# Set-up of a fused recurrence and highway layer: identity folded into the raw weights, diagonals on GpSimd, weight scaling on ScalarE, y parts of the last outputs issued ahead, another order list

## The chip, the cores and the metric

The kernel runs on one core of one Trainium2 chip. The metric is the device time of one execution in microseconds. A profiled execution also gives a span, from the first to the last recorded instruction; the time is a little longer than the span.

Names in the profile: PE is TensorE (PEld its weight loads), DVE is VectorE, ACT is ScalarE, POOL is GpSimd, SP is SyncE, whose queue here issues all the large transfers.

## The reference

Two layers follow each other on 4 x 6336 tokens of 256 channels, all in float32:

```python
sig = 1 / (1 + exp(-f_logit))
f = lower_bound + (1 - lower_bound) * sig
for t in range(S):                       # per batch row, h starts at 0
    h = f[:, t] * h + (1 - f[:, t]) * x[:, t]
    y[:, t] = h
H = maximum(y @ w_h, 0)
T = 1 / (1 + exp(-(y @ w_t + b_t)))
out = T * H + (1 - T) * y
```

With u = 1 - sig = sigmoid(-f_logit) and c = 1 - lower_bound, per channel, f is 1 - c u and (1 - f) x is c u x. Since the recurrence is linear, the kernel scans b = u x instead of c u x; its y is then the true one divided by c, and c has to come back in the weights (both matrices are multiplied by c, row by row) and in the output.

The output is y + T (H - y). With H - y = max(y w_h - y, -y), the kernel takes w_h with the identity subtracted, so that a matmul gives y (w_h - I), and builds d = max(that, -c y), then d T, then the output as c y + d T.

## The kernel before

**Tiling.** The 25344 tokens are cut into 28 units, numbered 0 to 27, of 2, 2, 4, then 23 times 8, then 4 and 2 blocks of 128 tokens. Two halves of 128 channels (h or m, 0 and 1) are worked on separately. For each unit there are these steps, each a function `do_<letter>`:

- `l`, `x`: load the logits and x by SP (line 244), 1 MB each for a unit of 8 blocks
- `u`: u = sigmoid(-l), ScalarE (L256), tokens on partitions
- `b`: bv = u x, on GpSimd, or on VectorE where the token carries a `v` (L264)
- `i`: transposes of u into PSUM, TensorE (L271); `f`: f = 1 - c u out of PSUM, on ScalarE (L282) or, with `v`, on VectorE (L280)
- `p`: transposes of bv, TensorE (L291); `s`: the scan, VectorE (L308), which takes its start value from the scan of the unit before
- `z`, `g`: the two matrix products, TensorE (L320, with repeated blocks through the helper at L114)
- `t`: T = sigmoid(z + b_t), ScalarE (L333); `d`: max, VectorE (L337); `e`: d T, GpSimd or with `v` VectorE (L343)
- `o`: output in PSUM, tokens on partitions again, TensorE: c y by a product with a diagonal matrix `diag` (L365), plus d T by a product with the identity (L366)
- `c`: copy out of PSUM, ScalarE (L378) or with `v` VectorE (L376); `w`: store by SP (L382)

A token such as `b3.1v:0` means: step b of unit 3, part 1, on VectorE, in buffer slot 0. A step `k*3` is three matmuls of zeros on TensorE whose result nobody reads (L125, L114).

**Order.** Nothing chooses the order at run time. The long string `order` lists all steps; they are issued in that order and pinned (`pin`), so that each engine, SP too, works through its part of the list from front to back, waiting where an input or a buffer is not ready. An instruction that waits holds up all that stands behind it on its engine.

**Set-up steps.** `wt`, `wh` load the weights into `w_raw`; `pc`, `pb` turn lower_bound and b_t onto partitions with TensorE; `cc` makes c and -c (`ncc`) on VectorE; `dg` makes `diag` (c on the diagonal) and `ndiag` (-c on the diagonal), four VectorE instructions; `WT` scales w_t by c into `w_sb`, two VectorE instructions; `WH` does the same for w_h and adds `ndiag` to the two square parts on its diagonal, four VectorE instructions; `cb` copies b_t. A variant `WTa` for ScalarE exists and is not used.

**Shared port.** `shared` (L178) is called for `b`, `e`, `dg`, `WT`, `WH`: the next such GpSimd instruction is made to wait for the last such VectorE instruction before it in the list.

The PSUM has slots a0 and a1 of one bank (transposes `i` and `p`) and b0, b1, b2 of two banks (products, outputs).

Of the kernel before, what the change touches and what calls it, by code (L numbers as in the profile page):

```python
# [58 lines left out]
p6.1:0 i8.1:1 z5.0:1 f8.1:0 x10:1 e4.1 t5.0:0 g5.1:0 i7.1:1 b8.0:1 s6.1 i7.0:0 d5.0:1 z5.1:1 l12:2 f7.1:1 p7.1:1 d5.1
f7.0:2 t5.1 b8.1 g6.0:2 p7.0:0 e5.1 k*3:0 o4.1:1 s7.1:0 z6.0:0 d6.0:2 s7.0 u9:1 b9.0:2 g6.1:2 c4.1:3 d6.1 i9.0:1  # L60
t6.0:1 b9.1 o4.0:1 u11:2 i9.1:0 f9.0v:1 c4.0:2 w4.0 e6.0v f9.1:2 g7.1:0 z6.1:2 k*3:1 e5.2v i8.0:1 z7.0:1 e5.0v t6.1
w4.1 f8.0:3 p8.1:0 d7.1:0 t7.0:0 g7.0:2 e6.1 p8.0:1 b11.0:3 o5.0:0 u10:1 c5.0:0 w5.0 x12:2 o5.1:1 c5.1:1 w5.1 s8.1:1
i11.1:0 z7.1:0 f11.1:0 s8.0 b11.1 l13:0 d7.0 p9.0:1 i10.1:0 z8.0:1 e6.2 b10.1:1 g8.1:2 t7.1 f10.1:3 p9.1:0 s9.0:2
o6.1:0 x13:0 i10.0:1 d8.1:1 s9.1 g8.0:2 t8.0:1 u12:3 o6.0:1 f10.0:1 c6.1:0 c6.0:2 b10.0 e7.0 i11.0:1 w6.0 p10.0:0 w6.1
f11.0:2 z8.1:0 t8.1 z9.0:1 t9.0:0 d8.0 g9.0:2 s10.0:3 i12.0:1 p10.1:0 l14:1 f12.0:1 d9.0:2 o7.0:0 g9.1:1 c7.0:1 x14:1
w7.0 s10.1 u13:1 o7.1:2 c7.1:3 w7.1 b12.0:2 l17:0 p11.0:1 d9.1 s11.0:0 z9.1:0 t9.1 i12.1:0 b12.1 l15:2 z10.1:1 g10.1:2
e8.0 t10.1:2 e9.0v b13.0:1 z10.0:0 f12.1:2 p11.1:1 b13.1 t10.0 o8.1:1 d10.1:0 p12.1:0 c8.1:0 o8.0:2 s11.1 u14:2
g10.0:0 d10.0 c8.0:2 b14.1:3 i13.1:1 e10.0 f13.1:0 g11.1:1 b14.0 z11.1:0 s12.1:1 d11.1:1 w8.0 t11.1:0 x15:0 w8.1
# [5 lines left out]
p15.1:1 s15.1 c12.1:1 b17.1:2 f16.0:2 z14.1:0 z14.0:2 p16.0:0 s16.0:1 c12.0:3 t14.1:1 t14.0 g14.0:1 d14.0 i16.1:1
w11.1 l19:1 u18:3 x18:0 b17.0 e14.0 g15.1:0 d15.1:2 z15.0:2 i17.1:0 x19:3 f16.1:0 b18.0:3 p16.1:1 f17.1:1 b18.1 l20:2
s16.1 o13.1:1 t15.0:0 p17.0:0 g15.0:0 w12.1 d15.0 c13.1:0 u19:1 b19.1:1 o13.0:2 p17.1:1 z15.1:1 c13.0:2 z16.0:0
s17.1:2 t15.1 t16.0:1 z16.1:2 s17.0 g16.0:1 w13.1 t16.1 i18.0:1 d16.0:0 g16.1:0 o14.0:2 i18.1:0 f18.0:0 d16.1 e15.0v
o14.1:1 p18.0:1 s18.0:3 u20:2 w12.0 z17.0:0 c14.0:0 c14.1:1 f18.1:1 g17.0:2 d17.0:1 z17.1:1 b19.0 t17.0:0 i19.1:0
# [344 lines left out]
```

## Time and profile before

| | us |
|---|---|
| median of 3 runs | 207.75 (207.75 to 211.6) |
| profiled execution, its own time | 207.88 |
| its span | 206.1 |

| engine | busy us | share of the span | instructions |
|---|---|---|---|
| TensorE | 192.6 | 93% | 1837 |
| VectorE | 194.5 | 94% | 159 |
| ScalarE | 191.9 | 93% | 192 |
| GpSimd | 173.8 | 84% | 93 |

The DMA moved 78.68 MB, at a mean of 382 GB/s over the span. The granted TensorE clock was 0.995 of full speed.

How to read it: busy time is the union of an engine's recorded instructions. Matmuls are pipelined and their recorded ends are modelled, so a full TensorE row does not mean that it could do no more. In a timeline a row gives start, length, engine, line, operation, output and inputs with their shape, and, in brackets, the idle time before it and what ended that. In the rows that group instructions, the numbers are the busy time, the mean of one in ns, and the idle time before them. "SPq" is SP's queue of transfers.

### The profile page before, as it was taken

The page shows a single profiled execution, that of the slowest core. Times are in us where ns is not written, and L with a number is a line of the kernel's source. Part 1 is how long each engine was busy: PE and PEld are TensorE (multiplying, and loading weights), DVE is VectorE, ACT ScalarE, POOL GpSimd, SP SyncE. Part 2 cuts the span into 40 slices and gives each one's busy share as a digit, 9 for nine tenths or more (in the row PEclk, how much of TensorE's full clock was granted, in tenths as well). Part 3 has the DMA queues.
Part 4 walks back from the last instruction along what each step waited for, and adds up shares of the span by engine and source line. Part 5 has one row for each costly group of instructions (what it writes and reads, how often), then busy time and mean ns, then how long its engine had stood idle before and what let it go on. Part 6 is the DMA issues. An engine that isn't in the chain of part 4 may idle for free.

```text
span 206.1 us, 4635 instructions
## 1 busy us (share of the span) xinstructions
PE 192.6 (93%) x1837; PEld 133.8 (65%) x1837; DVE 194.5 (94%) x159; ACT 191.9 (93%) x192; POOL 173.8 (84%) x93
## 2 busy tenths in 40 slices
PE   7798799799998999999999999999999999999991
PEld 2366465566685776676577576677758758776770
DVE  0899999999999999999899999999999999999972
ACT  4369999999999999999999999999999999999891
POOL 3036989789979997999999999799899999998840
PEclk9999999999999999999999999999999999999997
DMA  6999999999999999999999999999999999725396
GB/s 196 370 424 422 411 418 423 409 423 417 414 423 408 429 417 426 423 420 413 425 424 416 433 411 417 429 415 418 407 422 422 414 392 378 286 104 204 138 382 248
DMA packets 16125, 78.68 MB, mean 382 GB/s; under 512 B 1764, under 2 KB 2536, under 8 KB 10216
## 3 DMA queue, kind: packets, MB, share of 16 engines
q1 hardware_dynamic: 16096, 78.39, 93.6%
q8 instruction: 14, 0.23, 0.4%
q14 instruction: 7, 0.06, 0.1%
q10 hardware_dynamic: 8, 0.00, 0.0%
HBM read 52.43 MB, written 25.95 MB: 380 GB/s over the span
## 4 chain that ended last, share of the span: by engine, by line
PE 53%; ACT 14%; DMA 13%; DVE 10%; issue 6%; POOL 2%; SPq 1%; ACTq 0%; DVEq 0%; POOLq 0%
DMA x<-in_x_dram 9%; DVE y L308 8%; PE op L366 7%; PE bT L291 7%; PE op L365 7%; PE g L320 7%; PE z L320 6%; PE uT L271 6%; PE g L114 6%; PE z L114 6%; ACT o L378 4%; ACT f L282 4%; DMA out_dram<-o 4%; ACT t L333 3%; POOL bv L264 2%
## 5 line engine op out<-in xcount | busy, mean ns | idle before, releaser
L264 POOL TENSOR_TENSOR bv<-u,x 128x1024 bf16<-128x1024 f16 (+1 forms) x49 | 100.9, 2085 | 16.9 <-DVE bt L207 10.7
L308 DVE TENSOR_TENSOR_SCAN y<-f,y,bT 128x1024 bf16<-128x1024 f16 (+5 forms) x54 | 106.8, 1989 | 0.2 <-PE bT L291 0.2
L343 POOL TENSOR_TENSOR d<-d,t 128x512 bf16<-128x512 bf16 (+3 forms) x33 | 73.3, 2234 | 9.6 <-DVE d L343 4.2
L337 DVE SCALAR_TENSOR_TENSOR d<-y,ncc,g 128x1024 bf16<-128x1024 bf16 (+2 forms) x56 | 63.1, 1137 | 1.5 <-PE g L320 1.0
L333 ACT ACTIVATE t<-z,bt 128x1024 bf16<-128x1024 f32 (+2 forms) x56 | 58.9, 1088 | 1.3 <-PE z L114 0.7
L282 ACT ACTIVATE f<-uT,ncc 128x1024 f16<-128x1024 f16 (+2 forms) x51 | 55.4, 1098 | 3.4 <-PE uT L271 2.2
L378 ACT COPY o<-op 128x1024 f32<-128x1024 f32 (+2 forms) x55 | 52.1, 984 | 2.4 <-PE op L366 1.6
L256 ACT ACTIVATE u<-l 128x2048 f16<-128x2048 f32 (+2 forms) x28 | 49.8, 1781 | 2.8 <-DMA l<-in_f_logit_dram 2.7
L366 PE MATMUL op<-ident_b,d 128*128 128x128 bf16 x396 | 49.5, 219 | 0.6 <-DVE d L343 0.6
L365 PE MATMUL op<-diag,y 128*128 128x128 f16 x396 | 49.7, 219 | 0.1
L366 PEld LDWEIGHTS <-d 128*128 128x128 bf16 x396 | 44.0, 113 | 3.2 <-DVE d L343 0.7
L365 PEld LDWEIGHTS <-y 128*128 128x128 bf16 x396 | 44.2, 113 | 1.7
L320 PE MATMUL g<-y,w_sb 128*128 128x512 bf16 (+1 forms) x112 | 39.5, 367 | 0.9 <-DVE d L337 0.7
L320 PE MATMUL z<-y,w_sb 128*128 128x512 bf16 (+1 forms) x112 | 39.3, 367 | 0.4 <-ACT o L378 0.4
L291 PE MATMUL bT<-ident_f,bv 128*128 128x128 f32 x198 | 31.8, 277 | 4.3 <-DVE y L308 2.6
L114 PE MATMUL z<-y,w_sb 128*128 128x512 bf16 x92 | 34.9, 379 | 0.0
L114 PE MATMUL g<-y,w_sb 128*128 128x512 bf16 x92 | 34.9, 379 | 0.0
L320 PEld LDWEIGHTS <-w_sb 128*128 128x128 f16 x224 | 21.6, 98 | 17.5 <-issue 0.9
L271 PEld LDWEIGHTS <-u 128*128 128x128 f16 x396 | 26.3, 98 | 10.2 <-issue 2.6
L271 PE MATMUL uT<-ident_h,u 128*128 128x128 f16 x396 | 31.2, 220 | 1.6 <-DVE y L308 0.8
L291 PEld LDWEIGHTS bT<-ident_f,bv 128*128 128x128 f32 x198 | 22.4, 141 | 12.3 <-ACT f L282 3.0
L114 PEld LDWEIGHTS <-w_sb 128*128 128x128 f16 x184 | 18.0, 98 | 16.7 <-issue 1.8
(39 smaller groups left out, 58.7 us busy)
## 6 DMA issues: line engine op xcount, KB each, us to landing
out_dram<-o SPq DMA_DIRECT2D x48, 512.0 KB, 7.7
l<-in_f_logit_dram SPq DMA_DIRECT2D x23, 1024.0 KB, 12.0
x<-in_x_dram SPq DMA_DIRECT2D x23, 1024.0 KB, 13.4
l<-in_f_logit_dram SPq DMA_DIRECT2D x2, 512.0 KB, 7.5
...
l<-in_f_logit_dram SPq DMA_DIRECT2D x3, 256.0 KB, 2.9
x<-in_x_dram SPq DMA_DIRECT2D x3, 256.0 KB, 3.9
out_dram<-o SPq DMA_DIRECT2D x2, 256.0 KB, 16.3
```

Source lines behind the costliest of these rows:

```text
L114: return pe.add_instruction(mybir.InstMatmult(name=nc.get_next_instruction_name(), start_tensor_calc=start, stop_tensor_calc=stop, tile_si ...
L264: shared(pin(e.tensor_mul(st[n]["bv"][:, a:c].rearrange("p k d j -> p k j d"), st[n]["u"][:, 2 * a:2 * c].rearrange("p (k j) d -> p k j d" ...
L271: pin(nc.tensor.transpose(uT[:, j * P:(j + 1) * P], st[n]["u"][:, j, h * P:(h + 1) * P], ident_h))
L282: pin(nc.scalar.activation(to, of, AF.Identity, scale=ncc[:, h:h + 1], bias=1.0))
L291: pin(nc.tensor.transpose(words[:, k:k + g * (P - 1) + 1:g], pair, ident_f))
L308: pin(nc.vector.tensor_tensor_scan(y[:, c:e], st[n]["f", h][:, c:e], st[n]["bT", h][:, c:e], 0.0 if fresh else carry[h], op0=ALU.mult, op1 ...
L320: pin(nc.tensor.matmul(p[:, a:e], w, half(n, "y", ki)[:, a:e], start=ki == 0, stop=ki == NH - 1))
L333: pin(nc.scalar.activation(half(n, "t", m), st[n]["z", m][:, :tokens(n)], AF.Sigmoid, bias=bt[:, m:m + 1]))
L337: pin(nc.vector.scalar_tensor_tensor(half(n, "d", m), half(n, "y", m), ncc[:, m:m + 1], st[n]["g", m][:, :tokens(n)], op0=ALU.mult, op1=AL ...
L343: shared(pin(e.tensor_mul(st[n]["d"][:, a:c], st[n]["d"][:, a:c], st[n]["t"][:, a:c])), not eng)
L365: pin(nc.tensor.matmul(o, half(n, "y", h)[:, cols], diag[:, h], start=True, stop=False))
L366: pin(nc.tensor.matmul(o, half(n, "d", h)[:, cols], ident_b, start=False, stop=True))
```

## The change

- `WI` is new: two GpSimd instructions subtract the identity from the two square diagonal parts of the raw w_h. With that, c (w_h - I) is a plain scaling, and `ndiag` is gone.
- `WHa` and `WTa` replace `WH` and `WT`: two ScalarE instructions each, a copy with a scale.
- `dgp` replaces `dg`: `diag` alone, two GpSimd instructions.
- For units 26 and 27 a new step `q` issues the y products of an output part, which need only the scan; `o` then issues only the d T products. The loops over output blocks run with the halves outside, the blocks inside.
- The list is another one: the order of nearly all steps, slots, the places of the stores among the loads on SP, the place of unit 27's loads, and the marks `v` differ. The marks are gone from b2.1, c25.1, e0.0, e2.0, e2.1, e25.0, e25.2, e27.1, e4.0 and f1.1, and are new on b3.0, b4.1, c25.0, c26.0, c27.1, e1.1, e25.1, e27.0, e3.1, e4.1 and e4.2.

The beginning of the list before and after, and its end:

```diff
-l1:0 l0:1 x0:0 x1:1 k*3:a0 l2:2 wt wh x2:2 l3:3 x3:3 l4:4 pc:0 x4:4 u0:0 l27:1 l5:5 b0.0v:0 x27:0 x5:5 u1:1 cc l6:0
-k*3:1 i0.1:0 f0.1:0 dg i1.0:1 b1.0v:1 f1.0:1 k*3:1 k*3:a0 p0.1:1 s0.1:0 i0.0:0 u2:0 f0.0v:0 p0.0:1 s0.0 x6:1 l7:2
-k*3:a0 WT pb:0 k*3:a1 i2.0:0 p1.0:1 f2.0:0 WH k*3:1 s1.0:1 i2.1:0 b2.1v:0 g0.0:1 b2.0 i1.1:1 z0.1:2 f2.1:1 cb f1.1v:2
-z0.0:0 g0.1:a0 p1.1:1 t0.0:0 d0.0:0 k*3:1 d0.1 p2.0:0 s1.1 k*3:0 e0.0v z1.1:1 p2.1:1 t0.1 u3:0 l8:3 g1.1:0 x7:2 s2.0:2
-e0.1 d1.1:1 b3.0:0 z1.0:2 t1.0:0 i3.1:0 f3.1:0 o0.0:0 g1.0:2 c0.0:0 s2.1 d1.0 b3.1v g2.1:2 i3.0:0 d2.1:0 p3.1*3:1 t1.1
-e1.1 e1.0 k*2:0 w0.0 u4:1 z2.0:1 f3.0:1 z2.1:0 b4.0:1 s3.1:0 p3.0:0 o1.0:2 t2.1:0 u27:0 b4.1 c1.0:1 s3.0 w1.0 x8:3
+l0:0 u0:0 l1:1 k*3:a0 x0:0 x1:1 pc:0 l2:2 wh b0.0v:0 cc x2:2 u1:1 wt l3:3 k*3:a1 pb:1 x3:3 i0.1:0 i1.0:1 l4:0 k*3:2
+b1.0v:1 f1.0:0 x4:4 WI p0.1:1 f0.1:1 i0.0:0 f0.0v:2 l5:1 k*3:0 p0.0:0 s0.1:0 u2:0 i1.1:1 s0.0 k*3:0 f1.1:1 WHa p1.0:0
+p1.1:1 k*3:0 WTa s1.0:1 s1.1 x5:0 b2.0:0 g0.1*1:a0 g1.0:0 i2.1:1 g1.1:2 cb f2.1:0 d0.1:0 i2.0:0 d1.0:1 b2.1 z0.1:1
+t0.1:0 p2.1:1 dgp d1.1 f2.0:1 g0.0:0 s2.1:2 u3:0 z1.1:2 e0.1 p2.0:0 z0.0:1 k*3:a1 t1.1:1 t0.0 i3.0:1 f3.0:0 s2.0 d0.0
+b3.1v:0 z1.0:2 i3.1:0 b3.0v t1.0 g2.1:0 z2.1:1 e1.1v p3.0*2:1 e1.0 e0.0 t2.1:2 d2.1:2 f3.1:1 s3.0:3 k*2:1 o1.0:0
+p3.1:0 g2.0:1 o0.0:2 u4:0 c1.0:0 w1.0 c0.0:1 w0.0 l6:0 x6:1 l7:2 x7:2 z2.0:0 s3.1 e2.1 b4.0:0 b4.1v t2.0 i4.0:1 f4.0:0
...
-p27.1:0 e25.1 e25.2v z26.0:2 o25.0:0 o25.1:1 z26.1:a1 s27.1 g26.1:a0 t26.0:0 z27.0:2 c25.0:3 t26.1 c25.1v o25.2:0
-t27.0:1 o25.3:1 d26.1 g27.0:a0 w23.1 z27.1:a1 w24.1 w24.0 e26.0 c25.2:0 e26.1v o26.0:2 o26.1:0 d27.0:0 g27.1:a0 d27.1
-w25.0 c25.3 t27.1 e27.0 e27.1v o27.0:1 c27.0v:1 c26.0:2 o27.1:a0 c26.1 w25.1 w26.0 w27.0 c27.1:3 w27.1
+c24.1 g26.1:2 z26.0:a1 c24.3:1 e25.1v s27.1 o25.0:1 w23.1 c24.2 o25.1:0 d26.1 e25.2 z26.1:a0 w24.0 o25.3:2 t26.0:0
+c25.1:2 g27.1:a1 c25.0v o25.2:0 t26.1 e26.0 z27.1:1 q26.0:a0 d27.1:2 e26.1v z27.0:a1 w24.1 c25.3:3 w25.0 q26.1:2 c25.2
+o26.0 t27.1:0 c26.0v:0 t27.0 w25.1 o26.1 q27.1:0 e27.1 g27.0:1 d27.0 q27.0:1 e27.0v o27.0 o27.1 c27.0v:1 c26.1 w26.0
+w27.0 c27.1v:2 w27.1
```

The code:

```diff
-    def do_dg(slot):
+    def do_dg(slot, gpsimd=False):
         for h in range(NH):
-            pin(nc.vector.tensor_scalar(diag[:, h], ident_h, cc[:, h:h + 1], None, op0=ALU.mult))
-            last = pin(nc.vector.tensor_scalar(ndiag[:, h], ident_h, ncc[:, h:h + 1], None, op0=ALU.mult))
-        shared(last, False)
+            e = nc.gpsimd if gpsimd else nc.vector
+            last = pin(e.tensor_scalar(diag[:, h], ident_h, cc[:, h:h + 1], None, op0=ALU.mult))
+        shared(last, gpsimd)
+
+    def do_WI(slot):
+        for h in range(NH):
+            own = w_raw[:, 0, h, h * P:(h + 1) * P]
+            shared(pin(nc.gpsimd.tensor_sub(own, own, ident_f)), True)
...
+    def do_WTa(slot, k=1):
         for h in range(NH):
+            pin(nc.scalar.activation(w_sb[:, k, h], w_raw[:, k, h], AF.Copy, scale=cc[:, h:h + 1]))
+
+    def do_WHa(slot):
+        do_WTa(slot, 0)
...
-        for j in range(a, c):
-            lo = j0 * P + j - j0
-            cols = slice(lo, lo + g * (P - 1) + 1, g)
-            for h in range(NH):
-                o = op[:, j - a, h * P:(h + 1) * P]
-                pin(nc.tensor.matmul(o, half(n, "y", h)[:, cols], diag[:, h], start=True, stop=False))
-                pin(nc.tensor.matmul(o, half(n, "d", h)[:, cols], ident_b, start=False, stop=True))
+    def do_q(n, k, eng, slot):
+        op = two_banks(slot, "op").rearrange("p (j d) -> p j d", d=D)
+        for first, _, o, h, cols in outputs(n, k, op):
+            pin(nc.tensor.matmul(o, half(n, "y", h)[:, cols], diag[:, h], start=first, stop=False))
+        st[n]["op", k] = op
+
+    def do_o(n, k, eng, slot):
+        if n in (26, 27,):
+            for _, last, o, h, cols in outputs(n, k, st[n]["op", k]):
+                pin(nc.tensor.matmul(o, half(n, "d", h)[:, cols], ident_b, start=False, stop=last))
+            return
+        op = two_banks(slot, "op").rearrange("p (j d) -> p j d", d=D)
+        for _, _, o, h, cols in outputs(n, k, op):
+            pin(nc.tensor.matmul(o, half(n, "y", h)[:, cols], diag[:, h], start=True, stop=False))
+            pin(nc.tensor.matmul(o, half(n, "d", h)[:, cols], ident_b, start=False, stop=True))
         st[n]["op", k] = op
```

More of the change, by code (lines that the diff above doesn't have):

```diff
@@ L59 @@
[L59 to L68, printed above, removed]
@@ L74 @@
[L74 to L78, printed above, removed]
@@ L227, in do_WH @@
     def do_WH(slot):
-        for h in range(NH):
-            own = slice(h * P, (h + 1) * P)
-            rest = slice((1 - h) * P, (2 - h) * P)
-            pin(nc.vector.scalar_tensor_tensor(w_sb[:, 0, h, own], w_raw[:, 0, h, own], cc[:, h:h + 1], ndiag[:, h],
-                                               op0=ALU.mult, op1=ALU.add))
-            last = pin(nc.vector.tensor_scalar(w_sb[:, 0, h, rest], w_raw[:, 0, h, rest], cc[:, h:h + 1], None,
-                                               op0=ALU.mult))
-        shared(last, False)
+        do_WT(slot, 0)
     def rows(full, n, j0, j1):
```

83 lines of the change are left out of this document (50 added, 33 removed).

## The prediction

> **What bounds the kernel now.** First the page: one span, the engines' shares, and where in time they hold.
>
> ```profile
> span 206.1 us, 4635 instructions
> PE 192.6 (93%) x1837; PEld 133.8 (65%) x1837; DVE 194.5 (94%) x159; ACT 191.9 (93%) x192; POOL 173.8 (84%) x93
> ...
> DVE  0899999999999999999899999999999999999972
> ...
> GB/s 196 370 424 422 411 418 423 409 423 417 414 423 408 429 417 426 423 420 413 425 424 416 433 411 417 429 415 418 407 422 422 414 392 378 286 104 204 138 382 248
> ```
>
> PE, DVE, ACT and the DMA are all near 93%, so the shares don't choose between them. The busy time by stage does: stage, its length, then PE, PEld, DVE, ACT, POOL busy, granted clock, DMA share, GB/s.
>
> ```profile
> 20.00:40.00 20.00, 16.86 (x142) 10.72 (x140) 20.00 (x15) 19.97 (x20) 17.74 (x12) 1.00 1.02 415
> 120.00:150.00 30.00, 29.84 (x300) 21.38 (x299) 30.00 (x20) 30.00 (x29) 27.69 (x11) 1.00 1.01 416
> 180.00:195.00 15.00, 15.00 (x152) 10.62 (x151) 15.00 (x13) 13.70 (x18) 13.33 (x11) 1.00 0.38 150
> ```
>
> VectorE alone is full in all three. GpSimd and TensorE have holes; the DMA is full until about 172 us and then falls away, so the inputs are in some 30 us before the end. The timeline of VectorE (start, length, idle before it in brackets) shows how it begins:
>
> ```profile
> 5.52 0.73 DVE L264 TENSOR_TENSOR bv<-u,x 128x512 bf16<-128x512 f16 x1 [4.39 <-DMA x<-in_x_dram]
> ...
> 6.46 0.25 DVE L211 TENSOR_SCALAR diag<-ident_h,cc 128x128 f16<-128x128 f16 x1
> ...
> 7.19 0.72 DVE L264 TENSOR_TENSOR bv<-u,x 128x512 bf16<-128x512 f16 x1
> ...
> 9.86 0.59 DVE L217 TENSOR_SCALAR w_sb<-w_raw,cc 128x256 f16<-128x256 f32 x2
> ...
> 11.39 0.75 DVE L308 TENSOR_TENSOR_SCAN y<-f,y,bT 128x256 bf16<-128x256 f16 x1
> ...
> 17.59 0.46 DVE L337 SCALAR_TENSOR_TENSOR d<-y,ncc,g 128x256 bf16<-128x256 bf16 x1
> 17.96 1.75 DVE L264 TENSOR_TENSOR bv<-u,x 128x1024 bf16<-128x1024 f16 x1
> 19.61 0.73 DVE L337 SCALAR_TENSOR_TENSOR d<-y,ncc,g 128x512 bf16<-128x512 bf16 x1
> 20.33 4.58 DVE L308 TENSOR_TENSOR_SCAN y<-f,y,bT 128x1024 bf16<-128x1024 f16 x2
> ```
>
> and how it ends, with ScalarE's last copy:
>
> ```profile
> 197.35 0.69 DVE L376 COPY o<-op 128x512 f32<-128x512 f32 x1 [0.23 <-PE op L366]
> 198.21 0.75 DVE L337 SCALAR_TENSOR_TENSOR d<-y,ncc,g 128x512 bf16<-128x512 bf16 x1 [0.17 <-PE g L320]
> ...
> 200.87 0.48 DVE L337 SCALAR_TENSOR_TENSOR d<-y,ncc,g 128x256 bf16<-128x256 bf16 x1 [0.78 <-PE g L320]
> ...
> 202.07 0.43 DVE L376 COPY o<-op 128x256 f32<-128x256 f32 x1 [0.32 <-PE op L366]
> ```
>
> ```profile
> 202.63 0.37 ACT L378 COPY o<-op 128x256 f32<-128x256 f32 x1 [1.30 <-PE op L366]
> ```
>
> From 5.52 us to the tail VectorE runs one instruction straight after the other. Its only marked waits are four at the end, 0.23 + 0.17 + 0.78 + 0.32 = 1.50 us, all for TensorE. After the last copy (203.0) 3.1 us go to the last store. So I count VectorE's work, and ask where it will have to wait.
>
> **The change, part by part: VectorE's work.** Neighbours overlap by about 0.09 us (17.96 + 1.75 ends 0.10 after the next starts), so an instruction is worth its mean less 0.09. Means by form:
>
> ```profile
> L264 DVE TENSOR_TENSOR bv<-u,x 128x1024 bf16<-128x1024 f16 x1 | 1.8, 1753 | 0.0
> L264 DVE TENSOR_TENSOR bv<-u,x 128x512 bf16<-128x512 f16 x3 | 2.2, 721 | 4.4 <-DMA x<-in_x_dram 4.4
> L343 DVE TENSOR_TENSOR d<-d,t 128x1024 bf16<-128x1024 bf16 x6 | 4.5, 756 | 0.0
> L343 DVE TENSOR_TENSOR d<-d,t 128x512 bf16<-128x512 bf16 x5 | 2.0, 420 | 0.1
> L343 DVE TENSOR_TENSOR d<-d,t 128x256 bf16<-128x256 bf16 x2 | 0.6, 278 | 0.1
> L280 DVE TENSOR_SCALAR f<-uT,ncc 128x256 f16<-128x256 f16 x2 | 1.0, 476 | 0.1
> ```
>
> Taken off VectorE: the diagonals `dg`, 6.46 to 7.19 = 0.73; both weights `WT WH`, 9.86 to 11.39 = 1.53; and by the new `v` marks b2.1 0.63, f1.1 0.39, c25.1 0.60, e0.0 and e27.1 0.38, e2.0, e2.1 and e25.2 0.99, e4.0 and e25.0 1.33. Together 6.58 us. Put on it: b3.0 and b4.1 3.33, c25.0 and c26.0 1.20, c27.1 0.34, e1.1 and e27.0 0.38, e3.1, e4.1, e4.2 and e25.1 1.32. Together 6.57 us. **The work is the same**: the 2.26 us of set-up that leaves is given back as other work. Only waits can change the time.
>
> **The head.** What decides is `b3.1v`, the first VectorE instruction that needs unit 3. Ahead of it the new list has the old one's instructions, less dg, WT, WH, b2.1, f1.1 and e0.0: 0.73 + 1.53 + 0.63 + 0.39 + 0.19 = 3.47 us. Without a wait it would start at 17.96 - 3.47 = 14.49. But it needs x3, and u3 from ScalarE:
>
> ```profile
> 16.40 2.14 POOL L264 TENSOR_TENSOR bv<-u,x 128x1024 bf16<-128x1024 f16 x1 [0.72 <-DMA x<-in_x_dram]
> ```
>
> ```profile
> 14.11 1.91 ACT L256 ACTIVATE u<-l 128x2048 f16<-128x2048 f32 x1
> ```
>
> GpSimd's b3.0 waited until 16.40 for that transfer. In the new list the same bytes stand ahead of x3 on SP (the two weights and x2 only change places), so it lands at 16.4 again: 1.9 us of the 3.47 saved in front are dead. Those 3.47 us of other work are still to be done behind it. VectorE's end moves by (16.40 - 17.96) + 3.47 = **+1.9 us** at the least, if nothing else changes.
>
> ScalarE may make it later. WHa and WTa now stand ahead of f2.1, t0.1, f2.0 and u3.
>
> ```profile
> 3.05 0.43 SPq L187 DMA_DIRECT2D w_raw<-in_moe_w_t_dram  x1
> ```
>
> ```profile
> w_raw<-in_moe_w_t_dram SPq DMA_DIRECT2D x1, 256.0 KB, 6.2
> ```
>
> ```profile
> L333 ACT ACTIVATE t<-z,bt 128x256 bf16<-128x256 f32 x6 | 2.8, 478 | 0.5 <-PE z L320 0.5
> L343 POOL TENSOR_TENSOR d<-d,t 128x256 bf16<-128x256 bf16 x4 | 2.6, 672 | 4.0 <-DVE d L337 1.8 <-DVE bv L264 1.3 <-DVE d L343 0.9
> ```
>
> The gate weights landed at 3.05 + 6.2 = 9.25 us; now 0.79 MB more (w_h, x2) go ahead, at 370 to 424 GB/s 1.9 to 2.1 us: about 11.25. Two scalings of the size of the 478 ns row take 0.8, f2.1 0.6, t0.1 and f2.0 1.0, and in between z0.1 has to come from TensorE, some 1 us: u3 starts at 14.6 to 15.1 and ends at 16.5 to 17.0, against 16.02 before. I take b3.1v at 16.9: shift -1.06 + 3.47 = **+2.4**. WI and dgp, four GpSimd instructions of 128 columns, cost between 0.25 (VectorE's diag row) and 0.67 each (the 672 ns row for 256 columns); nearest is the lower half, 0.4, so 1.6 us. WI lies under the wait for u2 and f1.1, dgp under GpSimd's holes (17.74 of 20 us busy); if WI had no cover, WHa and g0.1 would be up to 0.5 later, which the wait for x3 covers.
>
> **Middle and tail.** From there the list holds the same kinds of work, so I cost its other permutations at nothing, VectorE's full row being the cover. In the tail the y halves (`q`) take TensorE work out from behind e26 and e27: o27.0 and o27.1 shrink from eight matmuls to four. The 0.32 us wait stays; some 0.2 of it and of the 0.78 can go. Against it c27.0 and c27.1 now follow each other on VectorE (0.34 more), where ScalarE's took 202.63 to 203.0 beside it; I set the two against each other but for 0.2. Tail: **-0.2**. e25.0 on GpSimd instead of VectorE is covered by the o24 parts.
>
> Sum: 206.1 + 2.4 - 0.2 = 208.3 us of span. The profiled execution took 207.88, 1.78 more than its span and 0.13 above the median 207.75, so **210.1 us**, 1.1% above the median. About 2% (203.6 to 211.9) is what a measurement of this kernel can tell from no change.
>
> **Rivals.**
>
> *The head gain comes through.* If x3 and u3 come a microsecond sooner and all 1.50 us of tail waits go, the shift is 2.4 - 1.0 - 1.5 = -0.1: 206.0, or 207.8 us. For it: `q` and the copies on VectorE aim at just those waits. Against: x3's 16.40 is a transfer in a full queue. A gain over 2% would need 4 us less than VectorE's own work allows. Chance 0.14, of it 0.04 under 203.6.
>
> *Stores hold up the loads (slower).* On SP, w1.0 and w0.0 now stand ahead of l6; before, l6 and seven more loads went first.
>
> ```profile
> 13.82 0.33 SPq L244 DMA_DIRECT2D l<-in_f_logit_dram  x1
> ...
> 24.55 0.99 SPq L382 DMA_DIRECT2D out_dram<-o  x2
> ```
>
> l6 went at 13.82, both stores at 24.55. Through x5 8.9 MB are issued; by the GB/s row (5.15 us a slice) they are through at 24.5. If the stores are ready then, little is lost. Each microsecond later empties the DMA by one. The point is about 26.5 us, as unit 6 has some 2 us of slack (its load is needed by GpSimd after b5). The outputs of units 0 and 1 now wait for e1.1v behind b3.0v, so 29 us is possible: 4.5 late less 2 is +2.5, that is 210.8 and 212.6 us. Chance 0.22.
>
> *VectorE and GpSimd meet at the port.* Behind two rows of the tail stands such a case:
>
> ```profile
> 186.65 2.30 POOL L343 TENSOR_TENSOR d<-d,t 128x512 bf16<-128x512 bf16 x2
> ```
>
> ```profile
> 188.48 1.02 DVE L343 TENSOR_TENSOR d<-d,t 128x1024 bf16<-128x1024 bf16 x1
> ```
>
> That 128x1024 product took 1.02 us, against the mean of 0.756, while GpSimd ran until 188.95. The list moves eight such products or bv's off VectorE and eight others on. If three or four of the new ones (e3.1, e4.1, e4.2, b4.1) each wait for most of a GpSimd instruction of about 1 us, it is +3.5: 211.8, or 213.6 us. Eight for eight speaks against it; chance 0.10. The Trainium skill, "SBUF — State Buffer", section "Who interferes with whom", says that a VectorE instruction with two SBUF inputs and a GpSimd one take turns, whichever starts first holding the port to its end. The 1.02 us agrees in kind, though 0.26 us is no whole instruction.
>
> *TensorE's clock falls in the head.* The new list drops most dummy matmuls between 12 and 15 us.
>
> ```profile
> L114 PE MATMUL idle<-zeros 128*128 128x512 bf16 x23 | 7.8, 423 | 0.0
> L153 PE MATMUL idle<-zeros 128*128 128x512 bf16 x3 | 1.5, 626 | 1.2 <-DVE zeros L150 1.2
> ```
>
> At the start a dummy took 626 ns, later 423. At 0.2 us more for each of some six links up to s2.0, b3.1v comes 1.2 later: 209.5, or 211.3 us. Chance 0.08. The Trainium skill, "TensorE: Matmul & The Clock Gate", Part 1, states a half clock after about 3.4 us of idleness; the granted clock here is 1.00 in all quoted stages, so no row of this case shows the drop.
>
> **How the numbers follow.** Forecast 0.46 (209 to 211.4 us), head gain 0.14, stores 0.22, port 0.10, clock 0.08. Faster 0.04; slower 0.22 + 0.10 = 0.32; within 2% the rest, 0.64. The range leaves out the best of the head gain and the worst of stores and port: 207.4 to 213.8 us.
>
> **What would show it.** VectorE should have waits of 2 to 3 us in all between 6 and 17 us, b3.1v at 16.4 to 17.1, the first 128x1024 scan (before: 20.33) at 20.9 to 21.5, and then no waits until about 197. Right stores: w0.0 issued before 26.5 and no hole in the GB/s row at slices 5 and 6. Wrong: b3.1v before 15.5 (x3 sooner), VectorE waits between 30 and 190 us of over 1 us in sum (the list), 1 us or more less from the last scan to the end (the tail), or a granted clock under 0.9 before 25 us.

## The result and the profile after

The changed kernel takes 208.71 us (median of 10 executions, 208.34 to 209.81), the kernel before, run beside it, 207.94 us. The ratio is 1.0047, with a 95% interval of 1.0025 to 1.007: slower by about half a per cent, where +1.1% was forecast. (The ratio is that of the mean times and leaves out one execution of the kernel before, 211.6 us, that fell in a slower state.) The time lies in the predicted range, the sign is right, the forecast change is more than twice too large. Two later pairings of the same two kernels gave 1.0013 (0.9981 to 1.0046) and 1.0029 (1.0006 to 1.0053).

The profiled execution took 208.4 us with a span of 206.6. The page of the changed kernel, its span, the engines and VectorE's row of slices:

```profile
span 206.6 us, 4611 instructions
...
PE 192.8 (93%) x1816; PEld 133.1 (64%) x1841; DVE 193.8 (94%) x150; ACT 193.0 (93%) x195; POOL 175.6 (85%) x97
...
DVE  0789999999999999999999999999999999999972
...
GB/s 186 402 423 416 407 405 422 419 386 423 420 417 412 429 417 423 423 425 413 420 420 416 429 414 422 410 423 423 416 424 417 418 423 374 288 56 203 182 359 223
```

Nothing in the shares tells what happened. VectorE's timeline does. The head of the changed kernel:

```profile
7.61 0.48 DVE L284 TENSOR_SCALAR f<-uT,ncc 128x256 f16<-128x256 f16 x1 [0.59 <-PE uT L275]
...
9.81 1.39 DVE L312 TENSOR_TENSOR_SCAN y<-f,y,bT 128x256 bf16<-128x256 f16 x2 [0.54 <-PE bT L295]
...
13.13 2.45 DVE L312 TENSOR_TENSOR_SCAN y<-f,y,bT 128x512 bf16<-128x512 f16 x2 [0.62 <-PE bT L295]
...
15.87 2.51 DVE L268 TENSOR_TENSOR bv<-u,x 128x1024 bf16<-128x1024 f16 x2
18.25 0.29 DVE L347 TENSOR_TENSOR d<-d,t 128x256 bf16<-128x256 bf16 x1
...
19.18 4.59 DVE L312 TENSOR_TENSOR_SCAN y<-f,y,bT 128x1024 bf16<-128x1024 f16 x2
23.68 1.31 DVE L268 TENSOR_TENSOR bv<-u,x 128x1024 bf16<-128x1024 f16 x1
24.86 0.75 DVE L341 SCALAR_TENSOR_TENSOR d<-y,ncc,g 128x512 bf16<-128x512 bf16 x1
```

The three waits sum to 1.75 us, where 2 to 3 were forecast. b3.1v and b3.0v follow at 15.87 without a wait and take 2.51 us for both, and the first scan of unit 3 starts at 19.18, 1.15 us ahead of the 20.33 of before. Of that lead little is left late in the kernel. The same two scans, those of unit 24 (an expectation below calls them unit 25), in the kernel before and in the changed one:

```profile
174.76 4.58 DVE L308 TENSOR_TENSOR_SCAN y<-f,y,bT 128x1024 bf16<-128x1024 f16 x2
```

```profile
174.53 4.57 DVE L312 TENSOR_TENSOR_SCAN y<-f,y,bT 128x1024 bf16<-128x1024 f16 x2
```

So the changed kernel is 0.23 us ahead at this point, and its span ends 0.5 us behind: 0.73 us are lost in the tail. The tail of the changed kernel on VectorE:

```profile
192.81 1.91 DVE L312 TENSOR_TENSOR_SCAN y<-f,y,bT 128x512 bf16<-128x512 f16 x2
...
195.50 0.73 DVE L347 TENSOR_TENSOR d<-d,t 128x512 bf16<-128x512 bf16 x1
...
197.87 0.69 DVE L392 COPY o<-op 128x512 f32<-128x512 f32 x1 [0.35 <-DMA out_dram<-o]
...
200.36 0.69 DVE L392 COPY o<-op 128x512 f32<-128x512 f32 x1 [0.86 <-PE op L377]
...
202.25 0.93 DVE L392 COPY o<-op 128x256 f32<-128x256 f32 x2 [0.38 <-PE op L377]
```

New there is the wait of 0.35 us for a store: c25.0 writes into the output buffer that the store w23.0 empties. SP's queue shows when that store went out, in the kernel before and in the changed one:

```profile
191.70 0.33 SPq L382 DMA_DIRECT2D out_dram<-o  x1
```

```profile
193.10 0.33 SPq L398 DMA_DIRECT2D out_dram<-o  x1
```

And the stretches 190 to 193, 193 to 196 and 196 to 203 us (PE, PEld, DVE, ACT, POOL busy; clock, DMA share, GB/s), before and changed:

```profile
190.00:193.00 3.00, 3.00 (x33) 2.10 (x31) 3.00 (x4) 2.13 (x3) 3.00 (x3) 1.00 0.16 64
193.00:196.00 3.00, 3.00 (x45) 2.61 (x43) 3.00 (x5) 2.96 (x6) 2.02 (x2) 1.00 0.51 201
196.00:203.00 7.00, 5.63 (x70) 4.39 (x68) 4.66 (x10) 5.59 (x12) 2.00 (x3) 1.00 0.97 384
```

```profile
190.00:193.00 3.00, 3.00 (x44) 2.55 (x42) 3.00 (x4) 2.60 (x3) 3.00 (x3) 1.00 0.00 0
193.00:196.00 3.00, 2.95 (x40) 2.44 (x39) 2.89 (x4) 2.82 (x6) 2.94 (x2) 1.00 0.71 272
196.00:203.00 7.00, 5.62 (x69) 4.39 (x67) 5.11 (x11) 4.48 (x9) 2.94 (x3) 1.00 0.94 374
```

In the changed kernel the DMA moves nothing from 190 to 193 us and then has to carry the stores together; from 196 us to the last copy it is nearly full in both.

### The profile page after: what moved, and what is told of

It reads as the page before. It is cut to its first block, busy times and chain, and to the rows that moved or that the text cites. A ratio compares the mean times of both kernels' runs of the same rounds, so it can differ in the third digit from the quotient of the medians.

```text
span 206.6 us, 4611 instructions
## 1 busy us (share of the span) xinstructions
PE 192.8 (93%) x1816; PEld 133.1 (64%) x1841; DVE 193.8 (94%) x150; ACT 193.0 (93%) x195; POOL 175.6 (85%) x97
## 4 chain that ended last, share of the span: by engine, by line
PE 39%; ACT 21%; DVE 12%; POOL 9%; DMA 9%; issue 8%; SPq 1%; DVEq 0%; ACTq 0%; POOLq 0%
DMA l<-in_f_logit_dram 7%; ACT f L286 7%; PE op L381 6%; PE op L382 6%; PE g L324 5%; DVE y L312 5%; ACT u L260 5%; ACT t L337 5%; PE bT L295 5%; PE z L324 5%; POOL bv L268 5%; PE uT L275 4%; POOL d L347 4%; PE z L115 4%; ACT o L394 4%
## 5 line engine op out<-in xcount | busy, mean ns | idle before, releaser
L268 POOL TENSOR_TENSOR bv<-u,x 128x1024 bf16<-128x1024 f16 (+1 forms) x48 | 97.5, 2058 | 5.7 <-DVE d L347 3.6
L347 POOL TENSOR_TENSOR d<-d,t 128x512 bf16<-128x512 bf16 (+3 forms) x34 | 76.1, 2253 | 13.1 <-DVE d L347 8.3
L337 ACT ACTIVATE t<-z,bt 128x1024 bf16<-128x1024 f32 (+2 forms) x56 | 57.5, 1079 | 1.5 <-PE z L115 0.7
L394 ACT COPY o<-op 128x1024 f32<-128x1024 f32 (+1 forms) x53 | 52.1, 1009 | 1.2 <-PE op L382 0.5
L381 PE MATMUL op<-diag,y 128*128 128x128 f16 x384 | 48.1, 219 | 0.3
L382 PE MATMUL op<-ident_b,d 128*128 128x128 bf16 x384 | 48.0, 219 | 0.1
L382 PEld LDWEIGHTS <-d 128*128 128x128 bf16 x384 | 42.8, 113 | 3.0 <-POOL d L347 0.4
L381 PEld LDWEIGHTS <-y 128*128 128x128 bf16 x384 | 42.9, 113 | 2.4 <-DVE d L341 0.2
L115 PE MATMUL z<-y,w_sb 128*128 128x512 bf16 x87 | 33.0, 379 | 0.0
L115 PE MATMUL g<-y,w_sb 128*128 128x512 bf16 x76 | 28.8, 379 | 0.1
```

What stands on the lines that cost most here:

```text
L115: return pe.add_instruction(mybir.InstMatmult(name=nc.get_next_instruction_name(), start_tensor_calc=start, stop_tensor_calc=stop, tile_si ...
L268: shared(pin(e.tensor_mul(st[n]["bv"][:, a:c].rearrange("p k d j -> p k j d"), st[n]["u"][:, 2 * a:2 * c].rearrange("p (k j) d -> p k j d" ...
L337: pin(nc.scalar.activation(half(n, "t", m), st[n]["z", m][:, :tokens(n)], AF.Sigmoid, bias=bt[:, m:m + 1]))
L347: shared(pin(e.tensor_mul(st[n]["d"][:, a:c], st[n]["d"][:, a:c], st[n]["t"][:, a:c])), not eng)
L381: pin(nc.tensor.matmul(o, half(n, "y", h)[:, cols], diag[:, h], start=True, stop=False))
L382: pin(nc.tensor.matmul(o, half(n, "d", h)[:, cols], ident_b, start=False, stop=True))
```

## The experiments

All ratios are against the kernel before, run on the same chip beside the experiment, with their 95% interval.

### What one bv costs: b3.0 on VectorE in the kernel before

```diff
-e0.1 d1.1:1 b3.0:0 z1.0:2 ... s2.1 d1.0 b3.1v g2.1:2
+e0.1 d1.1:1 z1.0:2 ... s2.1 d1.0 b3.0v:0 b3.1v g2.1:2
```

> The kernel before with b3.0 on VectorE, directly ahead of b3.1. Theory (port): the pair takes 2.4 to 2.5 us, 1.25 each, instead of 1.75 for one; the first scan of unit 3 moves from 20.33 to about 20.4 + (x3's landing at 16.3 allows a start at about 17.96), that is 17.96 + 2.4 + 0.65 = 21.0, GpSimd gains 2.1 us, time within 0.7 us of the kernel before. Rival (1.66 each): the pair takes 3.3 to 3.4, scan at 21.9, time 1.6 us above the kernel before (209.5).

Measured: 208.78 us, ratio 1.0038 (1.0016 to 1.006), 0.86 us above the kernel before beside it, a little more than the 0.7 expected. VectorE of this experiment:

```profile
18.05 2.52 DVE L264 TENSOR_TENSOR bv<-u,x 128x1024 bf16<-128x1024 f16 x2
```

Two of them take 2.52 us, 1.26 each. The one instruction of the kernel before took 1.75, and it began at 17.96 while GpSimd's b3.0 ran from 16.40 to 18.54; 18.54 + 1.17 = 19.71 is where it ended. So 0.49 us of the 1.75 were a wait for GpSimd inside the instruction. That is the rule of the Trainium skill that the prediction cited ("SBUF — State Buffer", "Who interferes with whom"), and this pair of rows agrees with it: the one that came second ran when the first had ended.

### The other way round: b3.0 back on GpSimd in the changed kernel

```diff
-b3.1v:0 z1.0:2 i3.1:0 b3.0v t1.0 g2.1:0
+b3.1v:0 z1.0:2 i3.1:0 b3.0 t1.0 g2.1:0
```

> The new kernel with b3.0 on GpSimd again, b3.1 left on VectorE. Theory (VectorE's bv waits at the port for GpSimd's bv): b3.0 takes 2.1 us on GpSimd from about 15.5, and b3.1 on VectorE runs until some 1.2 us after GpSimd's end, so takes over 1.6 us instead of 1.26, as the row of 1.75 us did in the kernel before. VectorE saves less than 1.2 us, the first scan of unit 3 starts at 18.5 to 19.3 instead of 19.18. GpSimd's start also shows when x3 is there. Rival (a bv costs VectorE 1.75 us by itself, the 1.26 has another cause, such as back-to-back issue of two): b3.1 stays at 1.25 whether GpSimd runs beside it or not, and the scan starts 1.2 us sooner, at 18.0.

Measured: 209.2 us, 1.0081 (1.0049 to 1.0113). GpSimd and VectorE of this experiment:

```profile
17.39 2.14 POOL L268 TENSOR_TENSOR bv<-u,x 128x1024 bf16<-128x1024 f16 x1 [3.31 <-DVE bv L268]
```

```profile
15.94 1.32 DVE L268 TENSOR_TENSOR bv<-u,x 128x1024 bf16<-128x1024 f16 x1
...
20.34 4.58 DVE L312 TENSOR_TENSOR_SCAN y<-f,y,bT 128x1024 bf16<-128x1024 f16 x2 [2.25 <-issue]
```

The kernel's own `shared` makes GpSimd's b3.0 wait for VectorE's b3.1v, so the two never ran at once and this run doesn't show the wait at the port. It shows two other things. b3.1v, alone here, takes 1.32 us with GpSimd idle, so that the short time of the run before doesn't come from two in a row, as its rival had it. And without b3.0v the scan starts at 20.34, 1.16 us later.

### The set-up back on VectorE

The two weights are scaled by VectorE (WH, WT) in the places of WHa and WTa; WI stays.

```diff
-... f1.1:1 WHa p1.0:0 p1.1:1 k*3:0 WTa s1.0:1 s1.1 x5:0
+... f1.1:1 WH p1.0:0 p1.1:1 k*3:0 s1.0:1 s1.1 WT x5:0
```

> The new kernel with the weights scaled on VectorE (four instructions of about 0.25 us, the identity still taken out by GpSimd; the second weight behind s1.1), the rest unchanged. Theory (unit 3's input is there by 15.9 us, so the head is VectorE's own chain): 0.5 us of the first weight falls into the wait of 0.54 ahead of s1.0, the second adds 0.5: bv of unit 3 starts at 16.2 to 16.5 instead of 15.87, time 0.3 to 0.7 us over the new kernel. Rival (the prediction's step: the input of unit 3 binds, so set-up work ahead of it is free on VectorE): bv of unit 3 as before at 15.9, time unchanged.

Measured: 210.43 us, 1.0108 (1.009 to 1.0127). VectorE of this experiment:

```profile
15.53 2.45 DVE L312 TENSOR_TENSOR_SCAN y<-f,y,bT 128x512 bf16<-128x512 f16 x2 [1.76 <-PE bT L295]
17.89 0.46 DVE L341 SCALAR_TENSOR_TENSOR d<-y,ncc,g 128x256 bf16<-128x256 bf16 x1
18.27 2.49 DVE L268 TENSOR_TENSOR bv<-u,x 128x1024 bf16<-128x1024 f16 x2
```

The scans of unit 2 wait 1.76 us and start 2.40 later, and b3.1v follows at 18.27 with no wait of its own, where 16.2 to 16.5 was expected. Some 0.5 us of this belong to the execution, whose loads came later: in loads_slots (below) w_h and x3 landed as late by the traces' landing times (9.33 and 16.32 us, here 9.30 and 16.31), and b3.1v started at 16.41. So the set-up on VectorE cost 1.9 us at that place, and 1.3 us (by the two ratios) to 1.7 us (by the medians, on different chips) of the whole time. It is not hidden by the wait for x3, as the prediction had it.

### Parts of the list: two halves, and w_h earlier

The new list up to f21.1 with the old order behind it, and the old list up to there with the new end; nine and fourteen buffer slots had to be changed at the seam.

```diff
-... p20.1:1 s20.1 f21.1:0 z19.0:0 g19.1:1 ...
+... p20.1:1 s20.1 f21.1:0 t19.1:0 o17.1:1 ...
```

> The new set-up and the new list up to f21.1, from there the old list's order and marks, without the q step (o whole for units 26 and 27). Theory (the new head is level or slightly ahead, the new end loses): the scans of unit 25 start at 174.5 us as in the new kernel, the end as in the old one, span 205.9, time 207.7 us, ratio to the kernel before 0.999. Rival (the loss sits in the head and middle, as the prediction had it, the end gains 0.2): span 206.8, time 208.6 us, ratio 1.004 or more.

> The old set-up and list up to that place, from there the new list with q. Theory (the end loses about 0.7 us): span 206.8, time 208.6 us, ratio 1.0035. Rival (the end gains 0.2): span 205.9, ratio 0.999.

Measured: 210.16 us, 1.0108 (1.0089 to 1.0128), and 214.55 us, 1.0308 (1.0283 to 1.0332). Both stall behind the seam, the second most: VectorE there, in the profile of its longest execution (217.49 us),

```profile
166.18 2.35 DVE L309 TENSOR_TENSOR_SCAN y<-f,y,bT 128x1024 bf16<-128x1024 f16 x1 [3.24 <-ACT f L283]
```

waits 3.24 us for ScalarE's f. These waits belong to neither kernel. A list that was cut and joined can't be split into the worth of its halves, so nothing follows.

In a third run the load of w_h goes ahead of l2:

```diff
-... pc:0 l2:2 wh b0.0v:0 cc x2:2
+... pc:0 wh l2:2 b0.0v:0 cc x2:2
```

> The new kernel with w_h loaded ahead of l2 instead of behind it, nothing else changed. Theory (the new head waits for w_h: GpSimd's WI, ScalarE's WHa and, behind it, f2.1 and the scans of unit 2): WI starts by 8.2 us in every run, the first scan of unit 2 at 12.9 to 13.2, the slower group goes, median 0.4 to 0.8 us under the new kernel. Rival (the two groups come from somewhere else, or u2 is later by what w_h is sooner): groups and median unchanged.

Measured: 209.29 us, 1.005 (1.0017 to 1.0083). WI starts at 7.47 instead of 8.41, but l2, now behind w_h, comes later by as much (u2 starts at 8.63 instead of 7.67), and the scans of unit 2 start at 13.49: no gain. The changed kernel beside it, once more:

> The new kernel itself, unchanged, on the same chip as the next three, to compare them with. Expected ratio to the kernel before 1.003 to 1.007, its times in two groups, 208.3 to 208.8 and 209.4 to 209.8 us, as in its ten first runs. Theory (first loads): which group a run falls in goes by when w_h lands (8.4 us in the profile with 208.4, 9.6 to 9.8 in those of 209 to 210).

Measured: 209.22 us, 1.0013 (0.9981 to 1.0046). Its times, 207.65 to 209.84 us, don't fall into the two groups that were expected, and with the run before the theory that w_h sets them has no support.

### The tail: y products, copies and buffers

Three single edits of the changed kernel: the step `q` left out; a fifth output buffer for c25.1 and c25.0, so that they need not wait for w23.0; and c26.0 (behind t27.0) and c27.1 moved to ScalarE.

```diff
-... z27.1:1 q26.0:a0 d27.1:2 ... q26.1:2 c25.2 o26.0 ... q27.1:0 ... q27.0:1 e27.0v
+... z27.1:1 d27.1:2 ... c25.2 o26.0:a0 ... e27.0v
```

> The new kernel without the step q: the y products of units 26 and 27 are issued with the d products again; the rest of the list is unchanged. Theory (TensorE is full in the end, so the step only moves its work, and what the last products save is given back by z27.0, o26.0 and g27.0 behind q): d27.0 as before the last copies, time within 0.3 us of the new kernel. Rival of the prediction (q saves 0.2 us): 0.2 us longer than the new kernel, last copy at 203.4 instead of 203.2.

```diff
-c25.1:2 g27.1:a1 c25.0v
+c25.1:4 g27.1:a1 c25.0v
```

> The new kernel with a fifth output buffer, used by unit 25's first half alone (c25.1, c25.0), which so has no store of unit 23 to wait for. Theory (the later o23.0 sends w23.0 at 193.1 instead of 191.7, and the copies c25.1 and c25.0 wait 0.45 and 0.35 us for it): both waits go, the end comes 0.3 us sooner, 0.2 to 0.4 us under the new kernel. Rival (TensorE sets the end, and the wait is only cover): the wait moves to the product o26.0 ahead of c26.0 (0.86 becomes 1.2), time unchanged.

```diff
-o26.0 t27.1:0 c26.0v:0 t27.0 ... c27.1v:2 w27.1
+o26.0 t27.1:0 t27.0 c26.0:0 ... c27.1:2 w27.1
```

> The new kernel with c26.0 and c27.1 on ScalarE again (c26.0 behind t27.0). Theory (c26.0 on VectorE stands between o26.0 and d27.0, and c27.1 behind c27.0): d27.0 starts as soon as g27.0 is there, about 200.6 instead of 200.99, and the last two copies run side by side, 0.35 sooner: last copy ends at 202.5 instead of 203.18, 0.5 to 0.7 us under the new kernel. Rival (g27.0 on TensorE is not there sooner): only the 0.35 of the last copy is gained.

Measured: without q 208.65 us, 1.0031 (1.0015 to 1.0046); fifth buffer 209.29, 1.0047 (1.0025 to 1.007); copies on ScalarE 209.05, 1.0047 (1.0027 to 1.0066). None gains. q is worth nothing that can be measured. With the fifth buffer (the profile is of its longest execution) the 0.35 us wait is gone, and the wait ahead of c26.0 grows from 0.86 to 1.36 us, while ScalarE waits 0.86 for another store. With the copies on ScalarE, c27.1 there waits 0.89 us for the store that holds its buffer. An edit that only moves a wait between buffers or engines leaves the stores as late as they were.

### The tail: the stores themselves

The first two runs leave out the stores w23.0, w23.1 and w24.0 in each kernel (1.5 MB, that is 1536 output rows, not the 384 that the expectation names); the third keeps all stores and sends w23.0 sooner: o23.0 takes the PSUM slot of g25.1 and goes ahead of it, and c23.0 goes ahead of f26.1.

```diff
-f26.0:1 g25.1:0 e23.0v d25.0:0 e24.0 i26.1:0 o23.0:2 ... d25.1 f26.1:3 s26.1 p27.0:0 e24.2 o24.0:0 c23.0:2
+f26.0:1 e23.0v o23.0:0 d25.0:0 g25.1:2 e24.0 i26.1:0 ... d25.1 c23.0:2 f26.1:3 s26.1 p27.0:0 e24.2 o24.0:0
```

> The changed kernel without the stores w23.0, w23.1 and w24.0: those 384 output rows of 256 columns (1.5 MB) are left out, everything else is done. Theory (the tail ends when the backlog of stores is through): the DMA no longer runs full from 194 us to the last copy, the last store follows its copy at once, and the time from the last copy to the end of the span falls from 3.4 to 3.0 us or less; the span is 0.4 to 0.8 us shorter, about 208.0 us. Rival (TensorE's chain g27.0, d27.0, e27.0, o27.0 sets the end): no more than 0.2 us less.

> The kernel before without the same three stores (1.5 MB of the output left out). Theory of the backlog: here the stores went out earlier (w23.0 at 191.70), so there is less to gain: 0 to 0.3 us, and the two kernels without these stores differ by 0.2 us or less in their tails. Rival: no change, and the difference of the tails stays 0.7 us.

> The changed kernel with o23.0 moved ahead of d25.0 and g25.1 (the PSUM slots of o23.0 and g25.1 exchanged) and c23.0 ahead of f26.1, so that w23.0 can go at about 192.0 instead of 193.10. Theory of the backlog: the idle gap of the DMA is filled for 1.1 us, and the end comes 0.3 to 0.6 us sooner, about 208.3 us, as long as d25.1 doesn't wait for g25.1. Rival (TensorE's chain): no change, or 0.2 to 0.5 us more where g25.1 comes late.

Measured: 208.32 us, 1.0014 (0.9981 to 1.0048); 208.99 us, 1.0063 (1.0029 to 1.0097); 208.34 us, 1.0018 (0.9998 to 1.0038). The head differs from execution to execution by more than the tail does, so the tails are read in the profiles, from the start of s26.1:

| kernel | s26.1 starts | last copy ends | span | to the last copy | from there to the end |
|---|---|---|---|---|---|
| before | 192.98 | 203.00 | 206.1 | 10.02 | 3.10 |
| changed | 192.81 | 203.18 | 206.6 | 10.37 | 3.42 |
| fifth_out | 193.77 | 204.46 | 208.1 | 10.69 | 3.64 |
| no_q | 193.65 | 203.66 | 206.6 | 10.01 | 2.94 |
| few_stores_new | 194.05 | 204.04 | 207.0 | 9.99 | 2.96 |
| few_stores_old | 195.79 | 205.81 | 209.1 | 10.02 | 3.29 |
| o23_early | 192.78 | 202.77 | 205.5 | 9.99 | 2.73 |
| after_again | 192.97 | 203.42 | 206.9 | 10.45 | 3.48 |
| after_third | 193.37 | 203.77 | 207.2 | 10.40 | 3.43 |
| both_fixes | 192.53 | 202.53 | 205.3 | 10.00 | 2.77 |

after_again and after_third are the changed kernel unchanged, both_fixes comes last below. The changed kernel repeats its tail: 13.79, 13.93 and 13.83 us from s26.1 to the end. Without the three stores it is 12.95, while the other kernel's isn't shorter without them (13.12 and 13.31): the backlog of stores costs something in the changed kernel, and no cost shows in the one before. o23_early keeps all stores and sends w23.0 sooner; with it some order on TensorE and two PSUM slots change too. SP's queue there (two stores in one row, w23.0 the first):

```profile
191.75 2.55 SPq L398 DMA_DIRECT2D out_dram<-o  x2
```

Its tail is 1.07 us shorter than the changed kernel's. The direction is surer than the size. With an edit in the head alone (wh_early, loads_slots, weights_vector, b30_gpsimd) the changed tail took 13.2 to 13.5 us, so some 0.5 us come and go without any edit in the tail; why is open. The rival, that TensorE's chain sets the end, holds for a part: in the rows whose copies don't wait long for a store, the last copy ends 9.99 to 10.02 us after s26.1 starts, in both kernels. What late stores add is 0.4 to 0.7 us ahead of the last copy, and the stretch behind it. VectorE in o23_early has no wait at c25.0:

```profile
197.21 0.68 DVE L392 COPY o<-op 128x512 f32<-128x512 f32 x1
```

Why the kernel before without three stores is slower in the median is open. Its profiled execution, its longest (210.9 us), falls behind before 43 us, far ahead of the edit (its granted TensorE clock was 0.75 from 24 to 28 us, 1.00 in the kernel before), so only its tail is read here. And no_q has the short tail too, though its median isn't lower; this one profile doesn't tell whether q delays the stores.

### The head: stores and loads on SP

l6, x6, l7 and x7 ahead of the stores w1.0 and w0.0, into free input buffers:

```diff
-x5:0 b2.0:0 ... d0.0 b3.1v:0 ... c1.0:0 w1.0 c0.0:1 w0.0 l6:0 x6:1 l7:2 x7:2 z2.0:0
+x5:0 l6:2 x6:1 b2.0:0 ... d0.0 l7:3 x7:2 b3.1v:0 ... c1.0:0 w1.0 c0.0:1 w0.0 z2.0:0
```

> The new kernel with the loads of l6, x6, l7 and x7 ahead of the stores w1.0 and w0.0 on SP, into buffers that are free by then (other slots for l6, l7, l8, l9, l27). Theory of the prediction's rival (stores hold up loads): the hole of the DMA between 25 and 30 us (338 to 404 GB/s) goes, l8 is there without the 0.26 to 0.6 us wait of u8 at 41 us, median 0.3 to 0.6 us under the new kernel. Rival (the loads have slack): the DMA is full earlier, and the time stays within 0.2 us.

Measured: 215.96 us, 1.0355 (1.0308 to 1.0403). ScalarE and VectorE of this experiment:

```profile
38.64 1.01 ACT L394 COPY o<-op 128x1024 f32<-128x1024 f32 x1 [7.15 <-DMA out_dram<-o]
```

```profile
41.61 1.28 DVE L341 SCALAR_TENSOR_TENSOR d<-y,ncc,g 128x1024 bf16<-128x1024 bf16 x1 [6.74 <-PE g L115]
```

The copy c2.0 reuses the buffer of w1.0, whose store now stands in the queue behind some 4 MB of loads: 7.15 us on ScalarE, and soon 6.74 on VectorE. A run with the same order, w_h early, the fifth output buffer and the copies on ScalarE together met the same wait (6.24 us) and took 215.54 us, 1.0326 (1.0276 to 1.0377):

> All together: w_h ahead of l2, l6 to x7 ahead of the first stores, the fifth output buffer for unit 25, c26.0 and c27.1 on ScalarE. If the three waits add, 207.0 to 207.4 us, ratio to the kernel before 0.995 to 0.998, the last copy at 202.0 to 202.4 us. If VectorE's work and TensorE's end bind as in the kernel before: ratio 1.000 or above.

So the same order was run again with other output buffers for c2.0, c3.0 and c3.1:

```diff
-c2.0:0 ... c3.0:1 ... c3.1:2
+c2.0:2 ... c3.0:3 ... c3.1:4
```

> loads_ahead (the loads of units 6 and 7 ahead of the stores w1.0 and w0.0) with other output buffers for c2.0, c3.0 and c3.1, a fifth one among them, so that no copy waits for w1.0 or w0.0. Theory (only the buffer behind the late store cost the 6.7 us in loads_ahead; the loads themselves are not short): back to the changed kernel's time within 0.5 us, 208.2 to 209.2. Rival (the loads of units 6 and 7 were late in the changed kernel): 0.5 us or more faster than it, below 208.0. If another copy now waits, 212 or more.

Measured: 208.24 us, 1.0016 (0.9993 to 1.0039), at the lower edge of the first expectation. The buffer explains all of the 7 us. The order of loads itself is worth half a microsecond at most, and the intervals of this run and of the changed kernel overlap.

### Both edits together

o23_early and loads_slots in one kernel, beside the unchanged new kernel on the same chip:

> The changed kernel unchanged, beside both_fixes on one chip. Both theories: 0.3 to 0.6% over the kernel before, about 208.7 us; s26.1 to the last copy's end 10.0 to 10.4 us, and 3.2 us or more from there to the end of the span.

> The changed kernel with the edits of o23_early and of loads_slots together. If late stores and the order of loads and stores cost what the single runs show (0.3 to 0.4 us each), 207.9 to 208.2 us, level with the kernel before (ratio 0.998 to 1.001) and 0.5 us or more under the changed kernel. Rival (both single runs were below the changed kernel by the spread of the head alone): no difference from the changed kernel beyond 0.2 us.

Measured: the changed kernel 208.81 us (208.15 to 210.22), 1.0029 (1.0006 to 1.0053); with both edits **207.59 us** (207.10 to 207.98), 0.9973 (0.9953 to 0.9994). This is faster than both kernels beside it, by 0.27% against the kernel before, and more than was expected (207.9 to 208.2). No execution with the edits was as slow as the fastest of the changed kernel: 1.22 us between the medians. Each edit alone (1.0018 and 1.0016) can't be told from the changed kernel by its ratio, so the two are shown together and not their shares. The tails, first of the unchanged kernel, then with the edits:

```profile
193.37 1.91 DVE L312 TENSOR_TENSOR_SCAN y<-f,y,bT 128x512 bf16<-128x512 f16 x2
...
198.47 0.69 DVE L392 COPY o<-op 128x512 f32<-128x512 f32 x1 [0.38 <-DMA out_dram<-o]
...
202.85 0.92 DVE L392 COPY o<-op 128x256 f32<-128x256 f32 x2 [0.38 <-PE op L377]
```

```profile
192.53 1.91 DVE L312 TENSOR_TENSOR_SCAN y<-f,y,bT 128x512 bf16<-128x512 f16 x2
...
196.97 0.68 DVE L392 COPY o<-op 128x512 f32<-128x512 f32 x1
...
201.77 0.76 DVE L392 COPY o<-op 128x256 f32<-128x256 f32 x2 [0.38 <-PE op L377]
```

With the edits the span is 205.3 instead of 207.2 in these two executions: 0.40 us less from s26.1 to the last copy (10.40 to 10.00), 0.66 less behind it (3.43 to 2.77), and 0.84 less ahead of s26.1. Of that 0.84 part is only the execution: x0 came 0.75 us sooner here, and the first scan of unit 3 started at 19.04 instead of 19.44, ahead of what the edit of the loads can do.

## Why the prediction was right in sign and wrong in size

The sum was 206.1 + 2.4 - 0.2 = 208.3 us of span; it is 206.6. Three terms failed: the price of the added bv and the wait for x3 and u3 were too high by 2.45 us together, the tail too low by 0.93. The sign came out right for another reason than was forecast: the head loses nothing once the first two are put right, and the loss came in the tail, for which a gain was forecast. That part is luck.

**The price of the added bv.** Here a term of the sum was mis-sized. The prediction took the one row of that form, 1753 ns, that is 1.66 us from start to start, for b3.0 and b4.1. Undisturbed it is 1260 ns (b30_vector). In the changed kernel the three of them took 3.56 us from start to start (15.87 to 18.25 and 23.68 to 24.86) where 3 x 1.66 = 4.98 were counted: **1.42 us** too much. "The work is the same" was false for this reason. The rival of the port had named the effect, as a price of the changed kernel, and quoted a row in which it showed; the row that it should have been looked for in was that of the price itself. In other executions a part of it comes back in b4.1v (last section).

**x3 and u3 as what binds the head.** b3.1v was put at 16.9, because x3 was to land at 16.4 again and u3 to end at 16.5 to 17.0. In the profiled execution it started at 15.87, **1.03 us** sooner. u3 came early; ScalarE of the changed kernel:

```profile
9.42 1.79 ACT L230 ACTIVATE w_sb<-w_raw,cc 128x256 f16<-128x256 f32 x4
...
13.38 1.91 ACT L260 ACTIVATE u<-l 128x2048 f16<-128x2048 f32 x1
```

All four scalings were done by 11.21, when the prediction let the gate weights only arrive (11.25), and u3 ended at 15.29. Nor does x3 land at the same time because the same bytes stand ahead of it: by the traces' landing times it came at 16.24 in the kernel before, and at 15.27, 15.57 and 15.93 in three profiles of the changed one. Stretch 5 to 10 us, before and changed:

```profile
5.00:10.00 5.00, 3.96 (x20) 1.75 (x18) 4.16 (x12) 2.16 (x4) 0.00 (x0) 1.00 1.03 364
```

```profile
5.00:10.00 5.00, 4.39 (x26) 1.93 (x25) 3.32 (x8) 2.87 (x7) 1.13 (x3) 1.00 1.06 400
```

The DMA moved 400 GB/s here, 0.18 MB more in 5 us, which is 0.45 us of the 0.97; the rest is open. b3.1v, at 15.87, followed what stands ahead of it on VectorE, not x3, and so it did in weights_vector.

The x3 half of this step was less wrong than one profile makes it look. In fifth_out, tail_act, few_stores_new, loads_slots, loads_ahead and new_then_old, whose heads are the same up to there, x3 landed at 16.26 to 16.60 us, and b3.1v started 0.09 to 0.10 us behind it, at 16.35 to 16.69; the work ahead of it on VectorE was as late. The u3 half failed in all six: u3 ended at 15.74 to 16.11.

With these two, 2.4 - 1.42 - 1.03 = -0.05 us at the end of the middle, and -0.23 was measured.

**The tail.** Forecast -0.2, measured +0.73. The step that failed is the one that costed the list's other permutations at nothing with VectorE's full row as the cover: o23.0 now stands behind g25.1 and z25.1, its store goes 1.4 us later, and neither VectorE nor TensorE covers a store. That late stores cost time here is shown in kind by few_stores_new, o23_early and the two edits together; how much of the 0.93 us is theirs is not, since edits in the head alone also shortened this tail. The 0.2 hoped for from q did not show (no_q). That c27.0 and c27.1 follow each other on VectorE costs little: both are done at 203.18, 0.18 behind before.

**The list.** That VectorE has no waits until about 197 held: it marks none between 16 and 197 us in the changed kernel. The small operations had nearly the right price: WI 0.43 each, dgp 0.59 each, where 0.4 was taken; GpSimd's long holes covered them.

**The rivals.** *The head gain comes through* was half right: at 174 us the shift was -0.23, close to its -0.1 for the whole, but its tail gain of 1.5 us did not come. *Stores hold up the loads*: both stores went at 21.52, before the 26.5 at which it was to decide, and slices 5 and 6 of the GB/s row read 407 and 405, no hole. (In the kernel before, l6 and four more loads went ahead of these stores, not l6 and seven.) What is left of it is a wait of u8 for its load of 0.26 us at 40.72 and at most the half microsecond of loads_slots. Its reverse is more than ten times dearer, as loads_ahead showed. *The port* shows in the changed kernel at 195.50, where a 128x512 product takes 0.73 instead of 0.42 us while GpSimd runs its own until 195.94; that is 0.3 us in place of 3.5, and in other executions up to 0.8 us more at b4.1v. *The clock* stayed at 1.00 in every stretch of the changed kernel quoted here, so it cost nothing in them.
